# Loading q and k over 128 partitions, a later assumed landing, and identity matmuls in TensorE's gaps: attention and a feed-forward stage on one core

## The chip, the cores and the metric

The kernel runs on one core of a Trainium2 chip. TensorE (PE) multiplies matrices into PSUM, ScalarE (ACT) and VectorE (DVE) do the rest of the arithmetic, SyncE (SP) issues the transfers, and GpSimd (POOL) is hardly used. The metric is the device time of one execution in microseconds (us): the median of three runs for the kernel before. A profile is one execution of its own, with its own time.

## The reference

Everything is float32, apart from the two weight matrices, which arrive as float64.

```python
def sm_attn(qq, kk, vv):
    s = scale * np.matmul(qq, kk.transpose(0, 1, 3, 2))
    s = s - np.max(s, axis=-1, keepdims=True)
    a = np.exp(s)
    a = a / (np.sum(a, axis=-1, keepdims=True) + 1e-09)
    return np.matmul(a, vv)

p_packed = sm_attn(p, k, v)                # 32 packed rows per head attend to 576
out = sm_attn(q, p_packed, p_packed)       # 576 rows attend to the 32
x = out.transpose(0, 2, 1, 3).reshape(B * S, H * D)
...
h = x @ w_in                               # 4608 x 512 times 512 x 2048
sp = np.where(h > 20.0, h, np.log1p(np.exp(np.minimum(h, 20.0))))
g = h * np.tanh(sp)
return (g @ w_out).astype(np.float32)      # times 2048 x 512
```

Batch 8, heads 8, sequence 576, head width 64, 32 packed rows.

## The kernel before

**The work.** The eight batches are handled one after another, each in two groups g of four heads. A batch's attention makes scores of the packed rows p against k (line 290, tile ps_s), their softmax, the product with v (line 413, ps_pp), its transpose ppT, then matches of q against ppT (line 290 again), a second softmax and transposes (lines 376, 377 and 507) into aT_hi and aT_lo, a high and a low half of float32 kept as fp32r (lines 564, 567). The feed-forward stage multiplies ppT into w_in first (pack, line 668, split into wp_hi and wp_lo at 680 and 685), so that its first product is wp times aT: 12 matmuls of line 748 for a *group* of 128 hidden columns, in two halves. ScalarE applies the gate (758, 760), the result is split into g_hi and g_lo (766, 770), and lines 800 to 802 multiply it with w_out in four column blocks and accumulate in PSUM. There are 16 such groups a batch; batch 0 does its first 8, batch 1 all 16, batch 0 the rest, then the others follow (TURNS, line 31). "First block" in this document means the first line-748 matmuls.

**The weights.** w_in and w_out come as pairs of 32-bit words. Each of 32 pieces is fetched (line 601, 512 KB, tile w_st), converted by two ScalarE steps (607, 611) and four VectorE steps (614, 620, 624, 630); a piece of w_out takes one more step on each (648, 651). Converted w_in is stored to memory and fetched again for later batches.

**The inputs of attention.** The host lays out q and k turned, so that the head width of 64 lies on partitions. A tile for four heads holds sequence positions 0 to 255 on partitions 0 to 63 and positions 256 to 575 on partitions 64 to 127 (PARTS, line 204). `load_turned` (262 to 267) fills it with two transfers, one for each half: 64 partitions with 256 KB and 64 with 320 KB. `products` (286 to 297) reads the two halves at lines 290 to 296. v comes as 512 KB on 128 partitions and a rest of 64 KB on 64 (lines 277, 278).

**The order of the work** is not left to the framework. `program` (827 to 1151) lists every step with its engine, a cost in ns, what it reads and writes, which buffers it takes, and a due time; `Lineup` (37 to 176) then simulates four engines (TensorE, VectorE, ScalarE and SP as the issuer of transfers) and puts every step where that simulation begins it. On the chip each engine works through its list in that order. For transfers `forward` keeps one wire: it runs at 385 bytes a ns (line 842), and a transfer's landing is assumed 500 ns after its last byte. For TensorE it doubles the costs for 4 us behind a gap of more than 2.5 us.

```python
                if begin - at["PE"] > 2500:
                    warm = begin + 4000
...
            if op["engine"] == "SP":
                wire = max(wire, begin + 1500) + op["lag"]
                ends[n] = wire + 500
```

LOADS (line 30) fixes the order of the first transfers: a weight piece, p, both k tiles of batch 0, a weight piece, v, and so on up to the second q tile and the sixth weight piece. Eight identity matmuls (lines 1156, 1157) come before everything else on TensorE; they write ps_warm, a PSUM tile of the bank with the tag ps_x (line 231).

Of the kernel before, what the change touches and what calls it, by code (L numbers as in the profile page):

```python
# [8 lines left out]
F32 = mybir.dt.float32  # L9
# [16 lines left out]
SLACK = 3.0  # L26
# [10 lines left out]
class Lineup:  # L37
# [3 lines left out]
    NEAR = 50  # L41
    HOP = 40
    AHEAD = 4000
    SWITCH = 1283
    STOP = 100
    ENGINES = ("PE", "DVE", "ACT", "SP")

    def __init__(self, slots):
# [51 lines left out]
    def forward(self, due):  # L100
        ops = self.ops
        free = {pool: [0.0] * n for pool, n in self.slots.items()}
        at = {e: 0.0 for e in self.ENGINES}
        wire, warm, table = 0.0, 0.0, "exp"
        begins, ends, tooks = {}, {}, {}
        left, left_users = [len(op["needs"] | op["behind"]) for op in ops], {k: set(v) for k, v in self.users.items()}
        pool_of, last = {}, {}
        est = {n: 0.0 for n, op in enumerate(ops) if not left[n]}
        while est:
            best = {}  # L110
            for n, begin in est.items():
                op = ops[n]
                begin = max(begin, at[op["engine"]])
                wanted = {}
                for pool, _ in op["takes"]:
                    wanted[pool] = wanted.get(pool, 0) + 1
                if any(len(free[pool]) < k for pool, k in wanted.items()):
                    continue
                for pool, k in wanted.items():
                    begin = max(begin, sorted(free[pool])[k - 1] + self.HOP)  # L120
                if op["engine"] == "SP":
                    begin = max(begin, wire - self.AHEAD, op["never_before"])
                cost = begin
                if op["table"] and op["table"] != table and due[n] > begin:
                    cost += self.SWITCH
                best.setdefault(op["engine"], []).append((cost, due[n], n, begin))
            if not best:
                raise RuntimeError("stuck: " + ", ".join(str(ops[n]["takes"]) for n in sorted(est)))
            picks = []
            for engine, found in best.items():  # L130
                first = min(found)[0]
                d, n, cost, begin = min((d, n, c, b) for c, d, n, b in found if c <= first + self.NEAR)
                picks.append((cost, d, n, begin))
            cost, _, n, begin = min(picks)
            op = ops[n]
            del est[n]
            took = op["cost"]
            tooks[n] = took
            if op["table"] and op["table"] != table:
                table = op["table"]  # L140
                begin += self.SWITCH
                tooks[n] += self.SWITCH
            if op["engine"] == "PE":
                if begin > at["PE"]:
                    took += self.STOP
                if begin - at["PE"] > 2500:
                    warm = begin + 4000
                if begin < warm:
                    took = min(2 * took, (took + (warm - begin) / 2) if begin + 2 * took > warm else 2 * took)
            begins[n] = begin  # L150
            at[op["engine"]] = begin + took
            if op["engine"] == "SP":
                wire = max(wire, begin + 1500) + op["lag"]
                ends[n] = wire + 500
            else:
                ends[n] = begin + took + op["lag"]
            for pool, k in op["takes"]:
                free[pool].remove(min(free[pool]))
                pool_of[k] = pool
            for k in op["uses"]:  # L160
                left_users[k].discard(n)
                last[k] = max(last.get(k, 0.0), ends[n])
                if not left_users[k]:
                    free[pool_of[k]].append(last[k])
            for m in op["after"]:
                left[m] -= 1
                if not left[m]:
                    est[m] = max((ends[w] + self.HOP for w in ops[m]["needs"]), default=0.0)
        assert len(begins) == len(ops), len(begins)
        return begins, ends, tooks  # L170

    def sequence(self, slack):
        begins, ends, _ = self.forward(self.dues(slack))
        for op in self.ops:
            op["begin"], op["end"] = begins[op["n"]], ends[op["n"]]
        return sorted(self.ops, key=lambda op: (op["begin"], op["n"]))


@with_exitstack
def body(  # L180
    ctx: ExitStack,
    tc: tile.TileContext,
    q_a: bass.AP,
    q_b: bass.AP,
    k_a: bass.AP,
    k_b: bass.AP,
    v_main: bass.AP,
    v_rest: bass.AP,
    pT: bass.AP,
# [5 lines left out]

    nc = tc.nc

    B, G, D, H4, CUT = q_a.shape  # L200
    NP = 32
    S = CUT + q_b.shape[4]
    HALF = S // 2
    PARTS = (0, CUT), (CUT, S)
    DF = w_in.shape[1]
    DO = w_out.shape[1]
    P = 128
# [14 lines left out]
    ps_h = ctx.enter_context(tc.tile_pool(name="ps_h", bufs=1, space=bass.MemoryType.PSUM))  # L222
# [5 lines left out]
    make_identity(nc, ident)  # L228


    ps_warm = ps_h.tile([P, P], F32, name="ps_warm", tag="ps_x")

    wo = {i: const.tile([P, 2, DO], F32R, name=f"wo{i}") for i in range(NF // 2)}

# [15 lines left out]
    class Batch:  # L250
# [10 lines left out]

        def load_turned(self, ts, src, g):
            ts[g] = att.tile([P, H4 * (S - CUT)], F32, name="xT", tag="T", bufs=XB)
            for u, (a, e) in enumerate(PARTS):
                nc.sync.dma_start(
                    out=ts[g][u * D:(u + 1) * D, :H4 * (e - a)].rearrange("a (h t) -> a h t", h=H4), in_=src[u][self.b, g]
                )

        def load_k(self, g):
            self.load_turned(self.kT, (k_a, k_b), g)  # L270

        def load_q(self, g):
            self.load_turned(self.qT, (q_a, q_b), g)

        def load_v(self, g):
            t = self.v[g] = att.tile([P, NCH + 1, H4, D], F32, name="v", bufs=VB)
# [547 lines left out]
            weights.append((t + LAG, WeightOut(f)))  # L824
    weights = [w for _, w in sorted(weights, key=lambda x: x[0])]

    def program():

        line = Lineup({
            "acc": 4, "ps_h": 1, "ps_x": 1, "ps_a": 1, "T": XB, "v": VB, "late": NF // 2, "wstage": 2, "w32": 4,  # L830
# [299 lines left out]
        for t in range(len(order) + LAG):  # L1130
# [17 lines left out]
            if t - 2 in paired:  # L1148
                left(t - 2)
        line.chain(LOADS)  # L1150
        return line

    with tc.manual_schedule(
        engines={mybir.EngineType.PE, mybir.EngineType.DVE, mybir.EngineType.Activation, mybir.EngineType.SP}
    ):
        for _ in range(8):
            nc.tensor.matmul(out=ps_warm, lhsT=ident, rhs=ident, start=True, stop=True)
        for piece in program().sequence(SLACK):
            piece["run"]()


# [13 lines left out]
def laid_out(q, k, v, p, moe_w_in, moe_w_out):  # L1175

    import numpy as np

    def turned(x, a, e):
        return by_slot(x)[..., a:e, :].transpose(0, 1, 4, 2, 3)  # L1180

    s = q.shape[2]
    cut = s // 128 * 64
    vs = by_slot(v)
    b, g, h, _, d = vs.shape
    main = s // 128 * 128
    ps = by_slot(p).transpose(0, 4, 1, 2, 3).reshape(b, d, g, -1)
    return {
        "q_a": turned(q, 0, cut),
        "q_b": turned(q, cut, s),  # L1190
        "k_a": turned(k, 0, cut),
        "k_b": turned(k, cut, s),
        "v_main": vs[:, :, :, :main].reshape(b, g, h, main // 128, 128, d).transpose(0, 1, 4, 3, 2, 5),
        "v_rest": vs[:, :, :, main:].transpose(0, 1, 3, 2, 4),
        "pT": np.concatenate([ps, ps], axis=1),
# [25 lines left out]
```

## Time and profile before

| | us |
|---|---|
| median of 3 runs | 734.15 |
| lowest and highest of the runs | 732.8, 736.47 |
| the profiled execution, whole | 735.77 |
| its span on the core | 734.0 |
| mean granted TensorE clock in the span | 0.976 |

The profile page gives busy times of the engines, the span in 40 slices, the DMA queues, the chain of work that ended last, and the costliest groups of instructions. Further views of the trace list instructions in order of time, the waits (who waited for whom, how long, how often, the longest), or busy times by stretch. A line such as "ACT wi L607 <- DMA w_st" says that ScalarE's step of line 607, writing wi, waited for the transfer into w_st. Times of instructions are from the start of the span; a matmul in float32 is recorded as two instructions.

By slices of 18.35 us, from the page (busy tenths, granted clock in tenths, GB/s moved):

| slice | PE | DVE | ACT | clock | GB/s |
|---|---|---|---|---|---|
| 1 | 6 | 4 | 4 | 7 | 266 |
| 2 | 6 | 5 | 4 | 5 | 276 |
| 3 | 7 | 8 | 8 | 7 | 320 |
| 4 | 9 | 9 | 8 | 9 | 171 |
| 5 | 9 | 9 | 7 | 9 | 6 |

### The profile page before, as it was taken

Reading aid. Unit: us, or ns where it says so; the run is one execution under the profiler, and the core shown is the slowest. Engines: PE = TensorE matmul, PEld = TensorE weight load, DVE = VectorE, ACT = ScalarE, POOL = GpSimd, SP = SyncE. Lnnn points to the kernel's source line nnn. Section 1 sums busy time; section 2 is a strip of 40 time slices with the busy share of each in tenths; the row PEclk is TensorE's granted clock in tenths of the full one; section 3 lists DMA queues with packets and bytes.
Section 4 is the critical chain, followed back from the end, with each engine's and each line's share of the span. In section 5 each row is a group of like instructions: output and inputs, shape, how many; then the busy total and the mean of one; then the engine's idle time right before and its main releaser. Section 6 shows DMA issues by size and latency. Waiting matters only on the chain.

```text
span 734.0 us, 12404 instructions
## 1 busy us (share of the span) xinstructions
PE 712.8 (97%) x5058; PEld 572.0 (78%) x5058; DVE 393.1 (54%) x702; ACT 301.3 (41%) x718; POOL 0.7 (0%) x6
## 2 busy tenths in 40 slices
PE   6679999999999999999999999999999999999997
PEld 4267787878787878887788787877788787888886
DVE  4589988955743446353743537343564445542332
ACT  4488776543521434243422425225333254332221
POOL 0000000000000000000000000000000000000000
PEclk7579999999999999999999999999999999999999
DMA  9994066732318310671115611292013911130002
GB/s 266 276 320 171 6 225 203 223 98 80 115 44 226 119 50 9 190 183 59 58 58 150 183 57 58 60 274 97 7 52 116 270 61 58 58 115 1 1 1 72
DMA packets 27833, 85.74 MB, mean 117 GB/s; under 512 B 3712, under 2 KB 5760, under 8 KB 27776
## 3 DMA queue, kind: packets, MB, share of 16 engines
q1 hardware_dynamic: 27776, 84.95, 38.4%
q8 instruction: 40, 0.66, 0.4%
q14 instruction: 17, 0.14, 0.1%
HBM read 71.30 MB, written 13.63 MB: 116 GB/s over the span
## 4 chain that ended last, share of the span: by engine, by line
PE 88%; DMA 8%; ACT 2%; DVE 1%; issue 0%; SPq 0%; ACTq 0%
PE ps_h L748 27%; PE acc L800 16%; PE acc L801 15%; PE acc L802 15%; PE ps_w L668 4%; DMA w_st<-in_w_in_dram 4%; PE ps_rest L800 2%; PE ps_rest L801 2%; PE ps_rest L802 2%; PE ps_pp L413 2%; DMA xT<-in_k_b_dram 2%; DMA xT<-in_q_b_dram 1%; DMA w_st<-in_w_out_dram 1%; PE ps_m L290 1%; PE ps_s L290 1%; PE ps_a L376 1%
## 5 line engine op out<-in xcount | busy, mean ns | idle before, releaser
L758 ACT ACTIVATE g<-ps_h 128x288 f32<-128x288 f32 (+1 forms) x256 | 98.5, 386 | 295.5 <-PE ps_h L748 212.2
L800 PE MATMUL acc<-wo,g_hi 128*128 128x512 f32 x512 | 203.9, 398 | 0.0
L801 PE MATMUL acc<-wo,g_hi 128*128 128x512 f32 x512 | 201.7, 394 | 0.0
L802 PE MATMUL acc<-wo,g_lo 128*128 128x512 f32 x512 | 201.1, 393 | 0.0
L748 PE MATMUL ps_h<-aT_hi,wp_hi 128*128 128x288 f32 x512 | 155.7, 304 | 0.3 <-DVE a L451 0.3
L748 PE MATMUL ps_h<-aT_hi,wp_lo 128*128 128x288 f32 x512 | 151.7, 296 | 0.2 <-DVE wp_lo L685 0.2
L748 PE MATMUL ps_h<-aT_lo,wp_hi 128*128 128x288 f32 x512 | 151.4, 296 | 0.0
L766 DVE CAST g_hi<-g 128x512 fp32r<-128x512 f32 x112 | 47.3, 422 | 180.5 <-ACT g L758 180.2
L748 PEld LDWEIGHTS ps_h<-aT_hi,wp_hi 128*128 128x128 f32 x512 | 96.6, 189 | 34.9 <-issue 24.2
L802 PEld LDWEIGHTS acc<-wo,g_lo 128*128 128x128 f32 x512 | 96.0, 188 | 23.0 <-DVE g_lo L770 0.2
L800 PEld LDWEIGHTS acc<-wo,g_hi 128*128 128x128 f32 x512 | 96.0, 188 | 19.6 <-DVE g_hi L766 3.4
L801 PEld LDWEIGHTS acc<-wo,g_hi 128*128 128x128 f32 x512 | 96.1, 188 | 11.0
L748 PEld LDWEIGHTS ps_h<-aT_lo,wp_hi 128*128 128x128 f32 x512 | 96.7, 189 | 9.0
L748 PEld LDWEIGHTS ps_h<-aT_hi,wp_lo 128*128 128x128 f32 x512 | 96.7, 189 | 0.6 <-DVE wp_lo L685 0.6
L770 DVE TENSOR_TENSOR g_lo<-g,g_hi 128x512 fp32r<-128x512 f32 x128 | 88.3, 690 | 6.4 <-ACT g_hi L766 0.4
L685 DVE TENSOR_TENSOR wp_lo<-ps_w,wp_hi 128x512 fp32r<-128x512 f32 x64 | 41.6, 684 | 40.7 <-ACT wp_hi L680 40.6
L680 ACT CAST wp_hi<-ps_w 128x512 fp32r<-128x512 f32 x64 | 34.5, 590 | 40.6 <-PE ps_w L668 40.6
L668 PE MATMUL ps_w<-wi,ppT 64*32 64x512 f32 x512 | 36.7, 615 | 0.0
L760 ACT ACTIVATE g_rest<-ps_h 128x64 f32<-128x64 f32 x128 | 28.0, 219 | 0.0
L800 PE MATMUL ps_rest<-wo,r_hi 128*128 128x512 f32 x64 | 25.1, 392 | 0.0
L801 PE MATMUL ps_rest<-wo,r_hi 128*128 128x512 f32 x64 | 25.1, 392 | 0.0
L802 PE MATMUL ps_rest<-wo,r_lo 128*128 128x512 f32 x64 | 25.1, 392 | 0.0
(97 smaller groups left out, 566.9 us busy)
## 6 DMA issues: line engine op xcount, KB each, us to landing
wi<-w_in_f SPq DMA_DIRECT2D x48, 512.0 KB, 4.8
w_st<-in_w_in_dram SPq DMA_DIRECT2D x16, 512.0 KB, 8.2
v<-in_v_main_dram SPq DMA_DIRECT2D x16, 512.0 KB, 8.4
w_st<-in_w_out_dram SPq DMA_DIRECT2D x16, 512.0 KB, 6.8
out_dram<-o SPq DMA_DIRECT2D x32, 256.0 KB, 2.2
xT<-in_k_b_dram SPq DMA_DIRECT2D x16, 320.0 KB, 6.4
xT<-in_q_b_dram SPq DMA_DIRECT2D x16, 320.0 KB, 8.9
xT<-in_k_a_dram SPq DMA_DIRECT2D x16, 256.0 KB, 5.5
```

Of the source, the lines that this page charges most:

```text
L290: nc.tensor.matmul(out=out[u][h * NP:(h + 1) * NP], lhsT=packT[u * D:(u + 1) * D, h * NP:(h + 1) * NP], rhs=xT[u * D:(u + 1) * D, h * (e - ...
L668: nc.tensor.matmul(out=ps[h * NP:(h + 1) * NP, g, :], lhsT=ppTb[row:row + D, g, h * NP:(h + 1) * NP], rhs=wis[c, g][row:row + D, h // 2, : ...
L680: nc.scalar.copy(out=hi, in_=fresh[b, c][:, g])
L685: nc.vector.tensor_tensor(out=lo, in0=fresh[b, c][:, g], in1=hi.bitcast(F32), op=ALU.subtract)
L748: nc.tensor.matmul(out=ps, lhsT=w[:, fs], rhs=a[:, g, cs], start=(n == 0), stop=(n == 5))
L758: nc.scalar.activation(out=self.act[:, hf * HALF:hf * HALF + m], in_=ps[:, :m], func=AF.Mish)
L760: nc.scalar.activation(out=self.g_rest[self.b % 2, self.f // 4][:, self.f % 4, :], in_=ps[:, m:], func=AF.Mish)
L766: cast(out=self.g[0], in_=self.act)
L770: nc.vector.tensor_tensor(out=lo, in0=self.act, in1=hi.bitcast(F32), op=ALU.subtract)
L800: nc.tensor.matmul(out=acc, lhsT=hi[:, cs], rhs=wh, start=start, stop=False)
L801: nc.tensor.matmul(out=acc, lhsT=hi[:, cs], rhs=wl, start=False, stop=False)
L802: nc.tensor.matmul(out=acc, lhsT=lo[:, cs], rhs=wh, start=False, stop=stop)
```

## The change

Three things change.

First, the layout and loading of q and k. The host now joins positions 0 to 255 (on rows 0 to 63) and the first 1024 of the 1280 columns of positions 256 to 575 (on rows 64 to 127) into one array of 128 rows, `q_main` or `k_main`, and keeps the remaining 256 columns of the second half as `q_rest` or `k_rest`. The tile on the chip holds the same values at the same places. It is loaded by one transfer of 128 partitions by 1024 columns (512 KB) and one of 64 partitions by 256 columns (64 KB).

Second, the planner's model. A landing is assumed 2000 ns after the wire, not 500. Costs of TensorE are doubled for 4 us behind a long gap only at TensorE's very first step.

Third, `sequence` fills TensorE's gaps in the plan. It goes through TensorE's steps in order of time, up to the first that takes the PSUM bank ps_h (the first block); where a gap is longer than 600 ns, it puts in identity matmuls, one for each 300 ns, until at most 600 ns are left. The gap ahead of the very first step isn't filled. The fills are like the eight matmuls at the start and write the same ps_warm, which now lies in the bank of ps_h. Their order among TensorE's steps is fixed; on the chip each runs when TensorE gets to it.

```diff
@@ class Lineup
+    FILL = 300
+    LATE = 2000
@@ forward
-                if begin - at["PE"] > 2500:
+                if begin - at["PE"] > 2500 and not at["PE"]:
                     warm = begin + 4000
...
-                ends[n] = wire + 500
+                ends[n] = wire + self.LATE
@@ sequence
-        begins, ends, _ = self.forward(self.dues(slack))
+        begins, ends, tooks = self.forward(self.dues(slack))
...
-        return sorted(self.ops, key=lambda op: (op["begin"], op["n"]))
+        fills, at = [], None
+        for op in sorted((op for op in self.ops if op["engine"] == "PE"), key=lambda op: op["begin"]):
+            if self.fill_until in [pool for pool, _ in op["takes"]]:
+                break
+            while at is not None and op["begin"] - at > 2 * self.FILL:
+                at += self.FILL
+                fills.append(dict(engine="PE", begin=at, end=at + self.FILL, n=len(self.ops), cost=0, run=self.fill, due=0, takes=[]))
+            at = op["begin"] + tooks[op["n"]]
+        return sorted(self.ops + fills, key=lambda op: (op["begin"], op["n"]))
@@ body
-    ps_warm = ps_h.tile([P, P], F32, name="ps_warm", tag="ps_x")
+    ps_warm = ps_h.tile([P, P], F32, name="ps_warm", tag="ps_h")
...
-            for u, (a, e) in enumerate(PARTS):
-                nc.sync.dma_start(
-                    out=ts[g][u * D:(u + 1) * D, :H4 * (e - a)].rearrange("a (h t) -> a h t", h=H4), in_=src[u][self.b, g]
-                )
+            nc.sync.dma_start(out=ts[g][:, :H4 * CUT], in_=src[0][self.b, g])
+            nc.sync.dma_start(out=ts[g][D:, H4 * CUT:], in_=src[1][self.b, g])
...
+        line.fill, line.fill_until = fill, "ps_h"
...
+        def warm():
+            nc.tensor.matmul(out=ps_warm, lhsT=ident, rhs=ident, start=True, stop=True)
+
         for _ in range(8):
-            nc.tensor.matmul(out=ps_warm, lhsT=ident, rhs=ident, start=True, stop=True)
-        for piece in program().sequence(SLACK):
+            warm()
+        for piece in program(warm).sequence(SLACK):
             piece["run"]()
@@ laid_out
+    def turned(x):
+        x = by_slot(x).transpose(0, 1, 4, 2, 3)
+        b, g, d, h, _ = x.shape
+        first, second = (y.reshape(b, g, d, -1) for y in (x[..., :cut], x[..., cut:]))
+        n = h * cut
+        return np.concatenate([first, second[..., :n]], axis=2), second[..., n:]
```

More of the change, by code (lines that the diff above doesn't have):

```diff
@@ L182, in body @@
     tc: tile.TileContext,
[L183 to L186, printed above, removed]
+    q_main: bass.AP,
+    q_rest: bass.AP,
+    k_main: bass.AP,
+    k_rest: bass.AP,
     v_main: bass.AP,
@@ L198, in body @@
     nc = tc.nc
-    B, G, D, H4, CUT = q_a.shape
+    B, G, D, LEFT = q_rest.shape
+    H4 = 4
     NP = 32
-    S = CUT + q_b.shape[4]
+    CUT = q_main.shape[3] // H4
+    S = 2 * CUT + LEFT // H4
     HALF = S // 2
@@ L263, in load_turned @@
             ts[g] = att.tile([P, H4 * (S - CUT)], F32, name="xT", tag="T", bufs=XB)
-            for u, (a, e) in enumerate(PARTS):
-                nc.sync.dma_start(
-                    out=ts[g][u * D:(u + 1) * D, :H4 * (e - a)].rearrange("a (h t) -> a h t", h=H4), in_=src[u][self.b, g]
-                )
+            nc.sync.dma_start(out=ts[g][:, :H4 * CUT], in_=src[0][self.b, g])
+            nc.sync.dma_start(out=ts[g][D:, H4 * CUT:], in_=src[1][self.b, g])
         def load_k(self, g):
-            self.load_turned(self.kT, (k_a, k_b), g)
+            self.load_turned(self.kT, (k_main, k_rest), g)
         def load_q(self, g):
-            self.load_turned(self.qT, (q_a, q_b), g)
+            self.load_turned(self.qT, (q_main, q_rest), g)
         def load_v(self, g):
@@ L825, in body, with program @@
     weights = [w for _, w in sorted(weights, key=lambda x: x[0])]
-    def program():
+    def program(fill):
         line = Lineup({
@@ L1177, in laid_out @@
     import numpy as np
-    def turned(x, a, e):
-        return by_slot(x)[..., a:e, :].transpose(0, 1, 4, 2, 3)
     s = q.shape[2]
     cut = s // 128 * 64
+    def turned(x):
[4 more added lines that the diff above has]
+        return np.concatenate([first, second[..., :n]], axis=2), second[..., n:]
+    q_main, q_rest = turned(q)
+    k_main, k_rest = turned(k)
     vs = by_slot(v)
@@ L1188, in laid_out @@
     return {
[L1189 to L1192, printed above, removed]
+        "q_main": q_main,
+        "q_rest": q_rest,
+        "k_main": k_main,
+        "k_rest": k_rest,
         "v_main": vs[:, :, :, :main].reshape(b, g, h, main // 128, 128, d).transpose(0, 1, 4, 3, 2, 5),
```

## The prediction

> **What bounds the kernel now.** I read the page's head first, then the engines' busy time by stretch, TensorE's waits after its first block of the second stage, the chain of waits ahead of that block, and last what ScalarE and VectorE wait for there.
>
> ```profile
> span 734.0 us, 12404 instructions
> PE 712.8 (97%) x5058; PEld 572.0 (78%) x5058; DVE 393.1 (54%) x702; ACT 301.3 (41%) x718; POOL 0.7 (0%) x6
> ```
> ```profile
> 0.00:47.16 47.16, 30.93 (x329) 17.32 (x329) 29.16 (x71) 23.72 (x55) 0.70 (x6) 0.67 0.99 275
> 47.16:734.00 686.84, 681.83 (x4734) 554.66 (x4730) 363.95 (x632) 277.54 (x663) 0.00 (x0) 1.00 0.35 106
> ```
>
> The columns of a stretch are its length, busy time of TensorE (PE), its weight loads, VectorE (DVE), ScalarE (ACT) and GpSimd, then granted clock, DMA share and GB/s. 47.16 is the start of the first matmul of line 748, the first block. From there TensorE is busy 681.83 of 686.84 us at a clock of 1.00: the change leaves that work as it is, so only a loss of a few us could be won in it. Ahead of it lie 47.16 us in which TensorE idles 47.16 - 30.93 = 16.2 us and runs at 0.67 of its clock, while the DMA engines are busy 0.99 of the time. The question is how much of these 47 us goes.
>
> ```profile
> 4.18 7.85 DMA w_st<-in_w_in_dram
> 12.04 9.80 DMA xT<-in_q_b_dram
> 21.86 11.87 DMA xT<-in_k_b_dram
> 33.75 9.82 DMA w_st<-in_w_in_dram
> 43.59 0.68 ACT wi L607
> 44.27 0.97 ACT a1T L400 x2
> 45.28 1.94 PE ps_pp L413 x80
> 47.23 3.05 PE ps_h L748 x12
> ```
>
> That is the chain of waits into the first block. From 4.18 to 43.57 it is four transfers end to end: a landing lets SP issue a later transfer, whose landing releases the next. Then a weight fetch (w_st) lands, ScalarE converts it (line 607), and only behind that, in ScalarE's order, copies the attention weights (line 400) for which TensorE waits. So the start is limited by transfers, and in its last step by the order in which ScalarE was told to work.
>
> **The transfers.** Each q or k tile comes as two transfers on 64 partitions each, 256 and 320 KB:
>
> ```profile
> xT<-in_k_b_dram SPq DMA_DIRECT2D x16, 320.0 KB, 6.4
> xT<-in_k_a_dram SPq DMA_DIRECT2D x16, 256.0 KB, 5.5
> v<-in_v_rest_dram SPq DMA_DIRECT2D x16, 64.0 KB, 8.0
> ```
> ```profile
> 0.00:6.00 6.00, 3.78 (x16) 3.48 (x16) 0.38 (x1) 2.35 (x3) 0.70 (x6) 1.00 0.69 187
> 6.00:18.00 12.00, 8.41 (x102) 3.78 (x106) 8.44 (x24) 5.76 (x16) 0.00 (x0) 0.62 1.03 307
> 18.00:30.00 12.00, 8.58 (x83) 2.71 (x73) 5.78 (x10) 5.25 (x14) 0.00 (x0) 0.50 1.03 240
> 30.00:54.00 24.00, 17.00 (x191) 13.75 (x197) 20.80 (x48) 16.95 (x41) 0.00 (x0) 0.73 1.03 321
> 54.00:84.00 30.00, 29.71 (x201) 23.25 (x184) 29.92 (x54) 26.35 (x54) 0.00 (x0) 1.00 0.30 119
> 22.00:30.00 8.00, 5.69 (x42) 1.59 (x43) 2.88 (x6) 3.39 (x10) 0.00 (x0) 0.50 1.03 229
> 50.00:54.00 4.00, 4.00 (x41) 3.56 (x48) 3.39 (x7) 3.91 (x12) 0.00 (x0) 1.00 1.02 407
> ```
>
> The last two rows are the pair to look at. The DMA engines are equally busy in both, but move 229 GB/s from 22 to 30 us, where mostly q and k tiles are in flight, and 407 from 50 to 54, where mostly weights move, which go to 128 partitions in rows of 4 KB. The new main transfer has the weights' shape (128 partitions, 4 KB each, 512 KB); the rest is 64 KB on 64 partitions. One tile (576 KB, 0.590 MB) now takes 0.590 / 229 = 2.58 us. Changed: the main part, 0.524 MB, at 407 takes 1.29 us, at the mixed rate of 321 1.63 us; the rest, 0.066 MB, at 229 takes 0.29 us. Saved are 0.66 to 1.00 us a tile; I take 0.83, halfway. From below the bound is nothing, if the slow stretch came from something other than the shape.
>
> [...]
>
> Six such tiles (k and q of batch 0, k of batch 1) are issued ahead of the weight fetch that lands at 43.57: 6 x 0.83 = **5.0 us** off the chain (4.0 to 6.0). The count of transfers stays at two a tile, so SP's queue holds no more than before. One small thing is later: the first four matmuls of a score waited for the 256 KB half alone and now wait for all 512 KB; at 407 against 229 GB/s these take 1.29 against 1.14 us, so 0.15 us a tile, inside the range above.
>
> **The planner's landings.** ScalarE's and VectorE's orders are fixed by the planner, which assumed a landing 0.5 us after the wire and now assumes 2.0. Weight conversions move back by up to 1.5 us in these orders, behind attention steps that are ready sooner.
>
> ```profile
> ACT wi L607 <- DMA w_st<-in_w_in_dram: 11.4, 5, 5.9
> ACT wo L607 <- DMA w_st<-in_w_out_dram: 6.7, 2, 5.2
> ```
>
> These are ScalarE's waits up to 47 us: 18.1 us standing in front of a conversion with other work queued behind it. Most of it would be idle anyway. On the chain the price is what stands behind the last such wait: the conversion 0.68 and the copies 0.97. I take **2.0 us** together with the earlier waits, bounds 0 and 4; if the conversions come too late instead, TensorE waits for weights (rival 1). Attention work moved forward on VectorE delays the conversions behind it by what it takes; it is the same work in total.
>
> **The fills.** Eight identity matmuls are timed in the trace already:
>
> ```profile
> 1.35 3.78 PE L1157 MATMUL ps_warm<-ident 128*128 128x128 f32 x16 [1.35 <-POOL ident masks.py:199]
> 47.80 0.44 PE L748 MATMUL ps_h<-aT_hi,wp_lo 128*128 128x288 f32 x1
> 48.04 0.44 PE L748 MATMUL ps_h<-aT_hi,wp_hi 128*128 128x288 f32 x1
> 51.03 0.29 PE L748 MATMUL ps_h<-aT_hi,wp_lo 128*128 128x288 f32 x1
> 51.16 0.29 PE L748 MATMUL ps_h<-aT_hi,wp_hi 128*128 128x288 f32 x1
> ```
>
> 3.78 / 8 = 0.47 us each at the low clock. Line 748's matmuls start 0.24 us apart at 48 us and 0.13 at 51, so at full clock a fill is about 0.47 x 0.13/0.24 = 0.26 us, against 0.3 in the plan. TensorE's idle time after the warm-up's own wait is 16.2 - 1.35 = 14.9 us, which bounds the fills at 14.9/0.3 = 50; the planner leaves up to 0.6 us in each gap, so I estimate 25. They run in waits and cost nothing while the real gaps are as long as the planned ones. Without that cover, 25 at the low clock cost 25 x 0.47 = 11.8 us. I take 0.5 us lost. What they buy: the first block's 12 matmuls at 0.13 instead of 0.24 apart, 12 x 0.11 = **1.3 us**; attention's matmuls on the chain would shrink too (up to half of line 413's 1.94), which I count only in the range, 0 to 4. That the planner no longer doubles a matmul's cost behind a long gap only reorders its list; I price that at nothing, bounds 1 us either way.
>
> So the first block comes 5.0 + 2.0 + 1.3 - 0.5 = 7.8 us earlier.
>
> **What is late next.** VectorE. In the stretch from 54 to 84 it is busy 29.92 of 30 us, and the weights come just in time:
>
> ```profile
> 56.52 0.65 DVE L651 TENSOR_TENSOR wo<-wo,wo 128x512 fp32r<-128x512 f32 x1
> 58.32 0.40 PE L800 MATMUL acc<-wo,g_hi 128*128 128x512 f32 x1
> 26.66 0.43 DVE L614 TENSOR_SCALAR wo<-wo 128x512 f32<-128x512 f32 x1 [4.62 <-ACT wo L607]
> ```
>
> The second output weight is ready at 57.17 and used at 58.32. An earlier block gains only as much as VectorE's work comes earlier, and that is the idle time it loses: up to 54 us it idles 5.6 (ahead of the first landing), 3.6, 6.2 and 3.2 us by the stretches above, 18.6 in all. The first 5.6 stay. Of the 6.2, 4.62 is one wait for a weight fetch behind q tiles; I let 5 go, with 1.5 of the 3.6 and 1 of the 3.2: 7.5 us. The smaller of 7.8 and 7.5 holds: span 734.0 - 7.5 = 726.5. The profiled execution took 735.77 in all, so 728.3; the runs' median, 734.15, lies 1.62 below the profiled one, hence **726.6 us**.
>
> **The rivals.** (1) VectorE takes the gain back: the weight fetches stay where they were in SP's order and only 2 us of its idle time go; TensorE then shows waits for g_lo, wo or wp_lo between 45 and 90 us: 732.1. For it speaks the slack of 1.15 us above, against it that its largest wait is itself for a transfer. (2) Slower: the fills stand in front of ready work. They run from the end of the matmul before them, not at a set time; if a transfer makes that matmul late, its fills come late too and hold up the next, independent step in TensorE's order. At 11.8 us, all on the chain and at the low clock, against 5.0 from the transfers and nothing else, the end is 6.8 us later: 741. It decides from 5.0/0.47 = 11 such uncovered fills. Against it: TensorE's real idle time was long, 14.9 us. (3) The fills don't hold the clock, so that part does not do what it says, and attention stays slow: 1.3 us and about 1 us of VectorE's earlier work are lost: 728.9.
>
> ```profile
> 15.00:18.90 3.90, 3.90 (x86) 2.61 (x85) 3.35 (x9) 2.66 (x8) 0.00 (x0) 0.50 1.06 302
> 33.00:36.00 3.00, 1.07 (x20) 0.15 (x8) 3.00 (x7) 1.48 (x3) 0.00 (x0) 1.00 1.03 361
> ```
>
> TensorE was busy all of 15 to 18.9 us, mostly with 64-column matmuls, and the clock stayed at 0.50; at 33 it was up. So being busy alone does not raise it, and gaps of up to 0.6 us stay. [...] (4) More is won: transfers no longer mix and all of VectorE's idle time but the first 5.6 and 1.5 goes, 11.5 us: 722.6.
>
> **How the numbers follow.** A measurement here tells about 0.5%, 3.7 us, from no change: faster is below 730.5, slower above 737.8. Chances: forecast 0.50, rival 1 0.17, rival 2 0.07, rival 3 0.15, rival 4 0.11. Faster are the forecast and rivals 3 and 4, 0.76; the same rival 1, 0.17; slower rival 2, 0.07. The range runs from 721.0 (a little under rival 4, as the fills' bound is open) to 733.5 (past rival 1); outside it lie rival 2 and the edges of 1 and 4, under 0.2.
>
> **What would show it.** Right: the first line-748 matmul near 39.5 us; 300 GB/s or more between 18 and 30 us; a granted clock of 1.00 in most stretches up to the first block, its matmuls 0.13 us apart; VectorE still full from some 46 us on, with less than 12 us idle before. Wrong: the same GB/s with k and q in flight; fills in front of a step whose inputs were long there; more than 2 us of TensorE's waits between the first block and 130 us, which would say that the order, not the transfers, decides.

## The result, and the profile after

The changed kernel takes 729.16 us (median of 5 runs, 728.33 to 730.39) against 734.69 before (5 runs, 732.8 to 736.69): a ratio of 0.992, 95% interval 0.9898 to 0.9943. The profiled executions took 728.70 and 735.77 us, with spans of 726.9 and 734.0. So the median fell by 5.5 us and the profiled span by 7.1: before's profiled execution lay 1.1 us above its median, the changed kernel's 0.5 below.

The busy times of the changed kernel by stretch, with the columns of before (length; busy time and count of TensorE, its weight loads, VectorE, ScalarE, GpSimd; granted clock, DMA share, GB/s):

```profile
0.00:39.22 39.22, 29.04 (x386) 20.04 (x386) 28.11 (x68) 23.71 (x55) 0.70 (x6) 1.00 0.98 326
39.22:726.90 687.68, 681.00 (x4737) 553.27 (x4730) 364.98 (x635) 278.41 (x663) 0.00 (x0) 1.00 0.31 106
0.00:6.00 6.00, 3.78 (x16) 3.49 (x16) 0.46 (x2) 2.47 (x3) 0.70 (x6) 1.00 0.67 205
6.00:18.00 12.00, 9.20 (x141) 5.69 (x141) 9.05 (x25) 6.39 (x18) 0.00 (x0) 1.00 1.02 342
18.00:30.00 12.00, 9.70 (x112) 5.42 (x113) 10.36 (x19) 7.44 (x18) 0.00 (x0) 1.00 1.04 351
30.00:54.00 24.00, 19.94 (x230) 15.40 (x229) 22.94 (x54) 20.38 (x48) 0.00 (x0) 1.00 1.03 382
54.00:84.00 30.00, 30.00 (x185) 24.36 (x184) 29.50 (x53) 24.57 (x52) 0.00 (x0) 1.00 0.04 11
```

The first block of the feed-forward stage starts at 39.22 us instead of 47.16, 7.94 us earlier; what lies behind it takes 687.68 instead of 686.84, so 0.84 us are given back there. From 18 to 30 us the DMA engines move 351 GB/s instead of 240 at the same share (1.04 and 1.03). The clock column says 1.00 in every stretch of this execution; over the five runs the span's mean was 1.00, 1.00, 0.999, 0.994 and 0.994, and the two last are the fastest and the slowest run. VectorE's idle time up to 54 us is 5.5 + 3.0 + 1.6 + 1.1 = 11.2 us instead of 18.6.

TensorE in order of time (start, length, engine, line): the eight identity matmuls at the start, the first two fills, the fills in the longest gap, then some of the first matmuls of line 759, which is line 748 of before.

```profile
1.35 3.78 PE L1169 MATMUL ps_warm<-ident 128*128 128x128 f32 x16 [1.35 <-POOL ident masks.py:199]
...
8.89 1.22 PE L1169 MATMUL ps_warm<-ident 128*128 128x128 f32 x4
...
27.96 3.62 PE L1169 MATMUL ps_warm<-ident 128*128 128x128 f32 x30
32.59 1.36 PE L518 MATMUL ps_t<-ident,a 128*128 128x128 f32 x8 [1.02 <-DVE a L561]
...
39.59 0.29 PE L759 MATMUL ps_h<-aT_hi,wp_lo 128*128 128x288 f32 x1
39.73 0.29 PE L759 MATMUL ps_h<-aT_hi,wp_hi 128*128 128x288 f32 x1
```

Thirty records are fifteen fills: 3.62 us, 0.24 each. The eight at the start are the same matmuls and take 0.47 each, twice as long, and the two at 8.89 take 1.22 together, although the clock column says 1.00 there too; the five at 11.07 take 1.38, 0.28 each. So up to about 10 us the column and the times of these matmuls do not agree. In the longest gap TensorE still waits 1.02 us behind them, so these fills held up nothing. The program has 29 fills. The matmuls of line 759 stand 0.13 to 0.14 us apart from the second on. The chain of waits, followed back from behind the first block, has this as its last transfer:

```profile
20.43 7.87 DMA w_st<-in_w_out_dram
```

In this view transfers lead the chain only to 28.30 us; later it runs through a step of VectorE that ended at 35.26, just before ScalarE began aT_hi. But ScalarE's own list shows that one more landing stands close ahead of the block:

```profile
34.69 0.69 ACT L618 ACTIVATE wi<-w_st 128x512 f32<-128x512 f32 x1 [0.57 <-DMA w_st<-in_w_in_dram]
35.28 0.56 ACT L575 CAST aT_hi<-ps_t 128x512 fp32r<-128x512 f32 x1
...
36.31 1.20 ACT L411 COPY a1T<-ps_a 128x512 f32<-128x512 f32 x2
```

From that landing on ScalarE works without a gap to the end of the copies of line 411, at 37.51, and TensorE waits 1.7 us for them. In before the end of the same list was this:

```profile
41.13 0.67 ACT L607 ACTIVATE wi<-w_st 128x512 f32<-128x512 f32 x1 [0.95 <-DMA w_st<-in_w_in_dram]
...
43.59 0.68 ACT L607 ACTIVATE wi<-w_st 128x512 f32<-128x512 f32 x1 [0.73 <-DMA w_st<-in_w_in_dram]
44.16 1.07 ACT L400 COPY a1T<-ps_a 128x512 f32<-128x512 f32 x2
```

There two conversions, each waiting for its weight piece, stood ahead of the copies; now only the first does. And TensorE's waits behind its first block, with their sum, count and longest, in before and now:

```profile
PE ps_h L748 <- DVE a L451: 0.3, 1, 0.3
PE ps_h L748 <- DVE wp_lo L685: 0.2, 1, 0.2
```
```profile
PE ps_h L759 <- DVE a L374: 1.0, 1, 1.0
PE acc L813 <- DVE g_lo L781: 0.7, 1, 0.7
PE ps_h L759 <- ACT g L769: 0.5, 1, 0.5
```

2.2 us now, 0.5 in before. The experiments show which part brings which.

### The profile page after: what moved, and what is told of

The parts are those of the page before. It is cut to its first block, busy times and chain, and to the rows that moved or that the text cites. A ratio compares the mean times of both kernels' runs of the same rounds, so it can differ in the third digit from the quotient of the medians.

```text
span 726.9 us, 12524 instructions
## 1 busy us (share of the span) xinstructions
PE 710.0 (98%) x5116; PEld 573.3 (79%) x5116; DVE 393.1 (54%) x702; ACT 302.1 (42%) x718; POOL 0.7 (0%) x6
## 4 chain that ended last, share of the span: by engine, by line
PE 88%; DMA 5%; DVE 4%; ACT 1%; SPq 0%; issue 0%; DVEq 0%; ACTq 0%
PE ps_h L759 27%; PE acc L811 16%; PE acc L813 15%; PE acc L812 15%; PE ps_w L679 4%; DMA w_st<-in_w_out_dram 4%; PE ps_rest L812 2%; PE ps_rest L811 2%; PE ps_rest L813 2%; PE ps_pp L424 1%; PE ps_m L301 1%; DMA v<-in_v_main_dram 1%; PE ps_s L301 1%; PE ps_a L387 1%; DVE wo L635 0%
## 5 line engine op out<-in xcount | busy, mean ns | idle before, releaser
L759 PE MATMUL ps_h<-aT_lo,wp_hi 128*128 128x288 f32 x512 | 150.9, 295 | 0.0
```

Of the source, the lines that this page charges most:

```text
L759: nc.tensor.matmul(out=ps, lhsT=w[:, fs], rhs=a[:, g, cs], start=(n == 0), stop=(n == 5))
```

## The experiments

My theory was that the transfers carry most of the gain, the later landing and the fills little each. The main rival gave it to the clock, a third to the order on ScalarE and VectorE. All kernels against the kernel before, measured beside them:

| kernel | first block, us | median, us | ratio, 95% interval |
|---|---|---|---|
| before | 47.16 | 734.69 | 1 |
| changed | 39.22 | 729.16 | 0.992 (0.9898 to 0.9943) |
| e1 transfers alone | 39.63 | 728.77 | 0.9917 (0.9903 to 0.9931) |
| e2 landing alone | 45.67 | 735.09 | 0.9992 (0.9978 to 1.0006) |
| e3 fills, with the rule for a cold TensorE | 44.06 | 734.20 | 0.9984 (0.9973 to 0.9994) |
| e4 changed, no fills | 41.29 | 729.24 | 0.9917 (0.9904 to 0.9931) |
| e5 changed, landing at 500 ns | 39.52 | 729.27 | 0.9924 (0.9905 to 0.9943) |
| e6 changed, old transfers | 44.88 | 736.47 | 1.0019 (1.0006 to 1.0032) |
| e7 changed, less on VectorE | 40.15 | 726.96 | 0.9891 (0.9875 to 0.9908) |
| e8 main part split by partitions | 43.77 | 735.73 | 1.0012 (1.0000 to 1.0024) |
| e8 main part split by columns | 38.41 | 728.45 | 0.9915 (0.9897 to 0.9932) |
| e9 changed, q ahead of a weight | 38.52 | 731.09 | 0.9943 (0.9929 to 0.9958) |
| e10 changed, landing at 4000 ns | 38.59 | 727.17 | 0.9893 (0.9878 to 0.9907) |
| e11 e1, q ahead of a weight | 33.55 | 732.48 | 0.9973 (0.9959 to 0.9987) |

The first block is that of the one profiled execution, the median that of all runs; before's own median beside e1 to e4 was 735.22, beside e5, e7 and e8 735.33, beside the rest 734.81.

### The transfers alone (e1)

```diff
 (the changed kernel)
-    LATE = 2000
+    LATE = 500
...
-                if begin - at["PE"] > 2500 and not at["PE"]:
+                if begin - at["PE"] > 2500:
...
-        return sorted(self.ops + fills, key=...)
+        return sorted(self.ops, key=...)
```

> The kernel before with q and k in the new layout alone: one transfer of 512 KB over 128 partitions and a rest of 64 KB; landings assumed at 500 ns, no fills, and the same order of instructions on every engine as before. My theory (the transfers carry most of the gain): 300 GB/s or more between 18 and 30 us instead of 240, first block 4 to 6 us earlier (41 to 43 us instead of 47.16), time 4 to 6 us under before, at a clock that is still 0.5 for most of the first 40 us. Rival (the clock carries it): the transfers are quicker but the start is held by TensorE at half clock and by the order on ScalarE, so the first block moves by less than 2 us.

```profile
0.00:39.63 39.63, 24.91 (x329) 15.54 (x329) 28.66 (x70) 23.48 (x55) 0.70 (x6) 0.83 0.97 330
18.00:30.00 12.00, 7.20 (x90) 2.80 (x89) 9.72 (x18) 7.17 (x18) 0.00 (x0) 0.97 1.04 351
```

In these stretches of e1 the transfers move 351 GB/s from 18 to 30 us, and the first block comes at 39.63 us, 7.5 us earlier, at a mean clock of 0.83 with its matmuls still 0.24 us apart. The time falls by 735.22 - 728.77 = 6.45 us: as much as in the changed kernel or a little more. On every engine the instructions stand in the order of before, so nothing but the transfers can have done it. My theory holds and its size was too small; the rival's bound of 2 us falls. The clock, which the expectation put at 0.5 for most of the first 40 us, was higher: 0.83 on the mean by that row.

### The landing alone (e2)

```diff
-                ends[n] = wire + 500
+                ends[n] = wire + 2000
```

> The kernel before with landings assumed 2000 ns after the wire instead of 500, nothing else. My theory: weight conversions stand later in ScalarE's and VectorE's order, so the last wait for a weight ahead of the first block no longer holds the attention copies; first block 0 to 3 us earlier (2.0 was taken), time 0 to 3 us under before. Rival (the order decides): 4 us or more.

The first block came 1.5 us earlier in the profiled execution, the time hardly moved: 0.9992, with 1 inside the interval. ScalarE's list ahead of the block ends as in before, so the later landing did not take the second conversion from in front of the copies. Its weight piece landed 1.4 us earlier (42.13 instead of 43.57); why was not separated:

```profile
42.15 0.67 ACT L607 ACTIVATE wi<-w_st 128x512 f32<-128x512 f32 x1 [0.41 <-DMA w_st<-in_w_in_dram]
42.73 1.06 ACT L400 COPY a1T<-ps_a 128x512 f32<-128x512 f32 x2
```

One wait further on takes part of it:

```profile
PE ps_h L748 <- DVE a L363: 1.1, 1, 1.1
```

The longest of TensorE's waits in e2 behind the first groups: a block waits for VectorE's step that takes batch 2's scores out of PSUM (line 363), at 153.8 us. In the changed kernel the same wait (line 374) is 1.0 us at 147 us; before, e1 and e4 do not have it. e4 has the changed kernel's plan without its fills, so the plan alone does not bring this wait; how early TensorE comes there counts too.

### The fills with the planner's rule (e3), and the change without the fills (e4)

e3 adds the fills and the planner's rule for a cold TensorE to the kernel before (in the diff of the change, all of `sequence`, `warm` and the condition in `forward`). e4 is the changed kernel with this:

```diff
-        return sorted(self.ops + fills, key=...)
+        return sorted(self.ops, key=...)
```

> The kernel before with the fills alone (29 identity matmuls and the planner's rule for a cold TensorE at its first step only), old transfers, landings at 500 ns. My theory: the clock stays up for more of the first 47 us, the first block's 12 matmuls stand 0.13 us apart, gain 1.3 us less 0.5 for fills in the way: 0.5 to 1.5 us under before. Rival (the clock carries the gain): 4 us or more under. Rival (fills stand in the way of late transfers): slower than before by up to 5 us.

> The changed kernel without the fills, all else the same, and the same order of the remaining instructions on every engine. My theory: clock near 0.5 up to the first block, whose matmuls stand 0.24 us apart; 0.5 to 2 us slower than the changed kernel, so 5 to 6 us under before. Rival (the clock carries the gain): 4 us or more of the gain is gone.

e3 gains 735.22 - 734.20 = 1.0 us, within the 0.5 to 1.5 expected; in the time neither rival holds. But e3 is not the fills alone. They are put in after the plan is made and touch TensorE's list only, while the rule changes the plan: in e3 ScalarE copies at 41.16 (line 409) and makes the second conversion behind that, at 42.40, as in the changed kernel and unlike before and e2. So it is the rule that moved this conversion, and no run has the rule alone. By stretch e3's clock is only partly up:

```profile
18.00:30.00 12.00, 8.48 (x82) 3.36 (x86) 8.56 (x16) 6.50 (x16) 0.00 (x0) 0.86 1.03 249
30.00:54.00 24.00, 20.91 (x225) 16.71 (x219) 20.70 (x49) 17.92 (x41) 0.00 (x0) 0.86 1.03 344
```

Landings are late there (249 GB/s), TensorE still waits for some of them, and the clock is 0.86 in both stretches; why it fell was not separated. The fills of the longest gap took longer than in the changed kernel:

```profile
32.50 6.07 PE L1167 MATMUL ps_warm<-ident 128*128 128x128 f32 x30
38.40 1.04 PE L516 MATMUL ps_t<-ident,a 128*128 128x128 f32 x8
```
```profile
35.76 1.36 DVE L559 TENSOR_TENSOR a<-a,small 128x512 f32<-128x512 f32 x2
```

Fifteen fills take 6.07 us instead of 3.62. VectorE had written what line 516 reads by 37.12, and TensorE began it at 38.40, right behind the fills: they held up ready work by 1.3 us, on the chain of waits into the block. This is the prediction's rival 2, small.

In the changed kernel's profiled execution, with the same 29 fills, the clock column says 1.00; in e4, without them, it says 0.58 from 6 to 18 us, 0.71 up to 30 and 0.79 up to 54. Yet e4 takes 729.24 us against 729.16, where I expected 0.5 to 2 us more. Its first block comes 2.1 us later, and its only wait of note behind the block is this:

```profile
PE ps_h L751 <- DVE a L454: 0.3, 1, 0.3
```

The two waits of 0.5 us for the gate (line 769) and 0.7 for g_lo (line 781) that the changed kernel has at its second and third steps are also in the profiles of e3, e5, e6, both e8 and e10, which have fills, and not in before, e1, e2 or e4, which have none; e7 and e9 have fills and other waits or none. The changed kernel waits 2.2 us behind its block and e4 0.3, with the same plan but for the fills: of the 2.1 us that the fills win at the block, 1.9 come back as waits for ScalarE and VectorE.

### Without the later landing (e5), without the new transfers (e6)

```diff
 (e5: the changed kernel)
-    LATE = 2000
+    LATE = 500
```

> The changed kernel with landings assumed at 500 ns again: new transfers and 29 fills. The first runs gave a first block at 39.63 us with the transfers alone, 39.22 in the changed kernel and 41.29 without fills. Theory now (with the quick transfers VectorE is full from about 24 us on and sets the first block, so neither fills nor landing move it): first block 38 to 40 us, time within 1 us of the changed kernel (728 to 730). Rival (the later landing costs what the fills win, both matter): first block below 38 us, 2 us or more under the changed kernel.

e6 is e3 with landings at 2000 ns.

> The changed kernel with the old transfers: landings at 2000 ns and the fills on the kernel before. Alone, the landing was worth 0.999 and the fills 0.998 of before. Theory (transfers carry the gain, and behind slow transfers the two others win little): 240 to 250 GB/s between 18 and 30 us, first block 43 to 45 us, ratio 0.996 to 1.000. Rival (the two together win what each can't alone): 0.993 or less.

e5: first block 39.52, time 729.27, as expected. So behind the new transfers the fills and the rule move the block by 0.1 us (39.63 in e1). The later landing and the rule without fills set it back to 41.29 (e4), and the fills make that up; these are single profiled executions. e6 is worse than either rival or theory said: 736.47, slower than before (1.0019, interval above 1). Its largest wait of TensorE behind the block is at the score of batch 2, 150.9 us:

```profile
PE ps_s L299 <- ACT g_rest L769: 2.8, 1, 2.8
```

ScalarE's step was named because it came last among what the profile sees; what in the plan puts the score there was not separated, and this profiled execution, 739.21 us, is the slowest of e6's twelve runs. Landing and fills alone are worth 0.999 and 0.998, together and behind old transfers they lose: they are not terms that add up.

### What made the old transfers slow (e8, two kernels)

```diff
 (the changed kernel; split by partitions)
-            nc.sync.dma_start(out=ts[g][:, :H4 * CUT], in_=src[0][self.b, g])
+            for u in range(2):
+                nc.sync.dma_start(out=ts[g][u * D:(u + 1) * D, :H4 * CUT], in_=src[0][self.b, g, u * D:(u + 1) * D])
...
 (split by columns)
+            for u in range(2):
+                cols = slice(u * 2 * CUT, (u + 1) * 2 * CUT)
+                nc.sync.dma_start(out=ts[g][:, cols], in_=src[0][self.b, g, :, cols])
```

> The changed kernel with the main part of each q and k tile as two transfers of 64 partitions by 4 KB (256 KB each) instead of one of 128 partitions; the rest of 64 KB stays, so three transfers a tile. Theory (the number of partitions sets the rate): between 18 and 30 us 240 to 270 GB/s again, first block 3 us or more later than 39.22. Rival (the old rows of 5 KB were slow, not the 64 partitions): 330 GB/s or more and a first block within 1 us of 39.22.

> The changed kernel with the main part of each q and k tile as two transfers of 128 partitions by 2 KB (256 KB each); three transfers a tile as in the run that splits by partitions. Theory (the number of partitions sets the rate): 320 GB/s or more between 18 and 30 us, first block within 1.5 us of 39.22. Rival (it is the number of transfers that counts, because each waits for one issued before): as slow as the split by partitions.

The same stretch, first of the split by partitions, then of the split by columns:

```profile
18.00:30.00 12.00, 8.46 (x71) 4.21 (x78) 7.38 (x13) 5.57 (x15) 0.00 (x0) 0.79 1.05 246
```
```profile
18.00:30.00 12.00, 11.03 (x120) 6.32 (x120) 10.27 (x19) 7.54 (x17) 0.00 (x0) 1.00 1.01 346
```

Both move the same bytes in the same number of transfers. Split by partitions the rate is 246 GB/s and the whole gain is gone (1.0012); split by columns it is 346 and the gain is all there (0.9915). So the low rate went with the 64 partitions of a transfer, neither with rows of 5 KB nor with the number of transfers. With the partitions the number of rows differs too, 64 of 4 KB against 128 of 2 KB a transfer; no run separates these two.

### VectorE relieved (e7)

```diff
 (the changed kernel, two steps of a weight piece)
-            nc.vector.tensor_scalar(out=self.dst, in0=self.dst, scalar1=F64_HIGH, scalar2=-F64_HIGH, op0=ALU.min, op1=ALU.max)
+            pass
...
-            nc.vector.tensor_tensor(out=bits, in0=bits, in1=self.r, op=ALU.add)
+            pass
```

This leaves out VectorE's clamp of every weight piece and the addition of its last bits.

> The changed kernel with two of VectorE's four steps of each weight piece left out: the clamp (0.42 us) and the last addition (0.69 us), so weights beyond float32's range and the lowest bits of all weights are not treated as they should be; the order of all else is the same. VectorE has 1.1 us less for each of 32 pieces. Theory (VectorE sets the first block): it comes 1.5 to 4 us earlier (35 to 37.7 us instead of 39.22), and the time falls by as much. Rival (transfers and the order on ScalarE set it): less than 0.7 us.

The stretches up to the first block and from 54 to 84 us (columns as above; VectorE is the third pair):

```profile
0.00:40.15 40.15, 30.61 (x387) 22.65 (x387) 23.63 (x59) 23.60 (x55) 0.70 (x6) 0.92 0.98 332
54.00:84.00 30.00, 30.00 (x185) 24.32 (x185) 23.86 (x40) 25.09 (x53) 0.00 (x0) 1.00 0.01 4
```

VectorE has 6.1 us in 30 to spare where it had 0.5, and the first block comes no earlier: 40.15. There the chain ends so:

```profile
26.12 8.38 DMA w_st<-in_w_in_dram
...
34.52 0.68 ACT wi L618
...
36.75 0.59 ACT a1T L411
37.39 2.83 PE ps_pp L424 x80
40.22 3.18 PE ps_h L756 x12
```

A weight landing at 34.50 stands ahead of the copies on ScalarE, as the one at 34.7 us does in the changed kernel. TensorE's clock was below 1 for a part (0.92 on the mean), and line 424's matmuls take 2.83 us instead of 1.73. So my expectation of an earlier block fell: in both executions the block waits for that landing and for ScalarE's list behind it, and VectorE's load does not set it.

Behind the block the profile of e7 has no TensorE wait at all, against 2.2 us in the changed kernel, and the median is 726.96, 2.2 us under the changed kernel's. But the two numbers do not belong together. The profiled execution is the slowest of e7's four, 728.47 us, with a span of 726.7 against 726.9. Its first block ran slowly, 12 matmuls in 3.18 us where the changed kernel's take 1.9 (39.22 to 41.08), which gives ScalarE and VectorE time. And the intervals of the two ratios overlap. So that VectorE decides what is given back is likely, above all for the wait for line 374 far behind the block, and not shown.

### A later order, and q ahead of a weight (e10, e9, e11)

```diff
 (e10: the changed kernel)
-    LATE = 2000
+    LATE = 4000
 (e9: the changed kernel; e11: e1)
-LOADS = [('fetch', 0), ('pT', 0), ('k', 0, 0), ('k', 0, 1), ('fetch', 1), ('v', 0, 0), ('fetch', 2), ('v', 0, 1), ('fetch', 3), ('q', 0, 0), ('fetch', 4), ('q', 0, 1), ('fetch', 5)]
+LOADS = [('fetch', 0), ('pT', 0), ('k', 0, 0), ('k', 0, 1), ('fetch', 1), ('v', 0, 0), ('fetch', 2), ('v', 0, 1), ('fetch', 3), ('q', 0, 0), ('q', 0, 1), ('fetch', 4), ('fetch', 5)]
```

> The changed kernel with landings assumed 4000 ns after the wire instead of 2000. Theory (the assumed landing hardly matters once transfers are quick): within 1.5 us of the changed kernel (727.7 to 730.7), first block 38 to 41 us. Rival (the order of conversions on ScalarE and VectorE decides): 2 us or more either way.

> The changed kernel with the second q tile of batch 0 loaded ahead of the fifth weight piece instead of behind it. The planner then also moves that piece's conversion on VectorE (2.3 us) behind the first softmax steps and the second batch's values behind the first block. Theory (the last q tile, then a VectorE that is full from about 24 us on, set the first block): q lands some 1.5 us earlier, first block 2 to 4 us earlier (35 to 37.2 us), time 1 to 3 us under the changed kernel (726 to 728), unless output weights then come too late for lines 811 to 813. Rival (VectorE's total work up to the first groups decides): first block earlier, but TensorE waits as much longer behind it, and the time is within 0.7 us of the changed kernel.

> The new transfers alone on the kernel before (landings at 500 ns, no fills), with the second q tile of batch 0 ahead of the fifth weight piece. Theory (transfers and their order decide, fills and landings do not): as the run that does the same to the changed kernel, within 1 us, so 726 to 728. Rival (with an earlier start the clock matters): 1.5 us or more slower than that run.

e10's waits of TensorE behind the first block, all of them:

```profile
PE acc L813 <- DVE g_lo L781: 0.7, 1, 0.7
PE ps_h L759 <- ACT g L769: 0.5, 1, 0.5
```

The wait of 1.0 us at line 374 is gone, and the time is 727.17: 2.0 us under the changed kernel's, more than the 1.5 I allowed and just at the bound of 2 that the rival, the order of conversions, had set. The intervals of the two ratios (0.9878 to 0.9907, 0.9898 to 0.9943) just overlap, and the two kernels were timed beside different runs of before, so that e10 is better than the changed kernel is likely and not shown; that it is better than before is. With 500, 2000 and 4000 ns (729.27, 729.16, 727.17) the time follows no slope; I take it that what counts is where the plan happens to put later steps, which was not tested.

e9 has its first block at 38.52, not much earlier, and takes 731.09, 1.9 us more than the changed kernel (the intervals just overlap): neither the 726 to 728 of my theory nor the rival's 0.7 us. The wait that came is the one that the expectation had named as its condition, the output weights:

```profile
PE acc L811 <- ACT wo L659: 2.5, 1, 2.5
PE acc L812 <- DVE wo L662: 0.2, 1, 0.2
```

It is not a late landing: from 30 to 60 us no wait of ScalarE in e9 is for a transfer, and its chain of waits into the first matmul of line 812 is mostly VectorE's steps, one behind the other:

```profile
46.66 0.34 DVE wi L631
47.00 0.64 DVE wo L662
47.69 0.59 PE acc L812
```

e11 shows the same more strongly. Its first block is the earliest of all, 33.55, 6.1 us ahead of e1's, and it still takes 732.48, 3.7 us more. What lies behind the first block, in e11 and then in e1:

```profile
33.55:729.60 696.05, 685.47 (x4822) 555.74 (x4820) 371.50 (x654) 284.10 (x680) 0.00 (x0) 1.00 0.32 108
```
```profile
39.63:726.70 687.07, 682.32 (x4736) 554.93 (x4730) 364.06 (x633) 277.53 (x663) 0.00 (x0) 1.00 0.32 106
```

Of the 9.0 us more, 3.15 are TensorE's own work: some attention that stood ahead of the block in e1 now comes behind it. The other 5.8 are idle time (10.6 against 4.75). Its longest waits:

```profile
PE ps_h L751 <- ACT g L761: 1.7, 1, 1.7
PE ps_h L751 <- ACT a1T L403: 1.3, 1, 1.3
PE ps_h L751 <- DVE aT_lo L570: 1.0, 1, 1.0
```

ScalarE's and VectorE's pieces were not there: VectorE was busy 23.68 of the 24 us from 30 to 54. So all that the earlier block won over e1 was given back, and more. Neither my theory nor its rival had this; the prediction's rival 1 had the mechanism.

## Why the prediction was right, and where its steps were not

The forecast held: faster, 729.16 in the range of 721.0 to 733.5. It named the right cause, the shape of the transfers. The gain was 5.5 us where 734.15 - 726.6 = 7.5 were forecast. That the span (726.9 against 726.5) and the first block (39.22 against about 39.5) came so close is luck: several steps that lead there were off and cancelled.

**The transfers were too small in the sum.** "Six such tiles ... 6 x 0.83 = 5.0 us off the chain (4.0 to 6.0)." Alone they brought the first block 7.5 us forward. The weight piece of the prediction's chain, which landed at 43.57, was the second of the two conversions ahead of the copies. In e1, with the same list, the first holds ScalarE, and the second no longer waits:

```profile
34.17 0.67 ACT L610 ACTIVATE wi<-w_st 128x512 f32<-128x512 f32 x1 [0.71 <-DMA w_st<-in_w_in_dram]
...
35.78 0.67 ACT L610 ACTIVATE wi<-w_st 128x512 f32<-128x512 f32 x1
```

The first piece landed at 34.15 instead of 41.11, 7.0 us earlier; the second had landed by 35.78, where ScalarE began its conversion without a wait, instead of at 43.57, 7.8 us earlier or more. If the six tiles brought all of that, it is at least 1.3 us a tile where 0.83 was taken. So the mis-sized step is the saving a tile, worked out from the rates of mixed stretches (229, 321 and 407 GB/s). Mixed stretches went faster elsewhere too: from 6 to 18 us, where weights and v move among the tiles, 353 GB/s in e1 instead of 307, from 30 to 54 us 382 instead of 321. Whether only the tiles were quicker there or also the transfers among them, these rows do not separate. That the rate went with the 64 partitions, and not with the count of transfers, e8 shows: 246 against 346 GB/s, with three transfers a tile in both.

**The landings were too large, and the order came from elsewhere.** "I take 2.0 us", bounds 0 and 4. Alone: 1.5 us at the first block, a ratio of 0.9992 in the time. Within the change: 0.3 us at the block (39.52 in e5) and nothing in the time. The step said that conversions move back "behind attention steps that are ready sooner". For the conversion ahead of the copies e2 does not show it, and e3 shows it with the old landing: the planner's rule for a cold TensorE moved it, which the prediction priced "at nothing". What that is worth by itself is open.

**The fills' term mixed two places.** 1.3 - 0.5 = 0.8 us went into the start of the block, but the 1.3 us are its 12 matmuls, which lie behind its start. At the start e3 measured 47.16 - 44.06 = 3.1 us for fills and rule, e4 2.1 for the fills within the change; in the time these were 1.0 and 0.1. So that 0.8 and 1.0 agree is luck. There are 29 fills, I estimated 25, each 0.24 us at full clock against my 0.26. Rival 2 came in e3, at 1.3 us. In the changed kernel it hardly shows: both transfers of the second k tile had landed by 9.6 us (issued at 3.36, 6.2 us under way), and its scores began at 10.04 behind two fills, up to 0.5 us later than these landings allowed, which no step of the chain contains. Rival 3 did not come in the profiled execution, where the first block's matmuls stood 0.13 us apart. But the fills do not always hold the clock: with them and the faster transfers the column says 0.72 from 6 to 18 us in e10 and 0.86 from 18 to 54 in e7, and with them and the old transfers 0.86 from 18 to 54 in e3.

**The sum** at the first block, 7.8 against 7.94 measured, agrees because the first term was 2.5 too small and the other two, 2.8 together, moved the block by only 0.4 us beside it (39.63 to 39.22).

**VectorE next.** Its idle time up to 54 us fell by 7.4 us, 7.5 predicted, and stretch by stretch 0.1, 0.6, 4.6 and 2.1 against 0, 1.5, 5 and 1. But "the smaller of 7.8 and 7.5 holds" made it a cap on the start, and e7 does not bear that out: with less work on VectorE a landing still held the block. What the prediction left out are waits behind the block: TensorE's idle time there went from 686.84 - 681.83 = 5.0 to 687.68 - 681.00 = 6.7 us, 1.7 more, of which 0.84 are left in the sum since TensorE had 0.83 us less to do there. Rival 1 was right as to kind and too large in size (732.1).

**From the span to the median.** "The runs' median, 734.15, lies 1.62 below the profiled one, hence 726.6." The changed kernel's profiled execution, 728.70, lies 0.46 below its median. One profiled execution against three runs was no offset to carry over; without this step the forecast was 728.3, 0.9 from the result: of the error of 729.16 - 726.6 = 2.6 us this step is 1.6.

**What would show it**: 351 GB/s (300 or more), clock 1.00 in the column and matmuls 0.13 us apart, 11.2 us idle on VectorE (under 12), 1.2 us of waits between the first block and 130 us (under 2): all as predicted. The wait of 1.0 us at 147 us lies behind that stretch.

What stays open: what the rule for a cold TensorE is worth alone, what moves line 374's wait in and out (e2, the changed kernel and both e8 have it, e4, e5 and e10 not), why e6 has 2.8 us at 150.9, and whether e7 and e10 are really better than the changed kernel.

## What to carry to other kernels

Bring a tile that feeds the start in by one transfer over all 128 partitions, and look at the GB/s of a stretch where the DMA engines show full: 240 against 351 at the same share went with the whole gain here. An earlier start counts only as far as the other engines can follow it (e11's block came 6.1 us before e1's, its end 3.7 us later): read TensorE's waits behind the point that moved, before and after, and its work on either side of it. Where a plan sets the order, compare the engines' lists before and after: here a rule priced at nothing took a conversion out of the way. Time each part alone and the whole without it, because parts that each look harmless (later landings, fills) lost time together and behind the old transfers (736.47 us against 734.81).

## What was not expected of the hardware

Two transfers to 64 partitions each, issued one behind the other, reached 246 GB/s in a mixed stretch where two of the same bytes to 128 partitions reached 346, with the DMA engines' busy share at 1.05 and 1.01. Half as many transfers again a tile, three instead of two, cost nothing that shows: 728.45 against 729.16 us. And TensorE's clock did not follow its busy share: in before it was busy for all of 15.0 to 18.9 us, and the clock stayed at 0.50, there and in the whole stretch up to 30 us; from 33 to 36 us it was busy for 1.07 of 3.00 us, and the clock was 1.00. What the clock follows, no run here separates.
